# Reordering masks, row sums and transposes in the attention part of a fused attention and expert kernel

## The chip, the cores and the metric

The kernel runs on one core of a Trainium2 chip. The metric is the device time of one execution in microseconds (us), less is better. Within one group of times executions repeat within about 0.4%, but the kernel before has two groups that lie 1.3 us apart, and this matters below. Three chips took part in the experiments, and one of them is slower in the part of the kernel that the change does not touch; kernels are therefore compared with runs of the kernel before on the same chip, or by stretches of the trace that the slow part does not reach. On that chip some executions were in a slower state (over 1.5% above the fastest of the same kernel): 5 of 27 of the kernel before, 1 of 14 of its repeat, and 2 of 6 of the new loop with the old start. Ratios use fast runs alone.

## The reference, cut to what matters

The reference is attention with a local window of 96 keys and 8 global keys, over 4 batches of 8 heads, followed by an assignment of tokens to 8 experts and their two matmuls.

```python
def _attn_ref(q, k, v, n_global, n_local):          # q, k, v: 4 x 8 x 768 x 64
    scores = scale * np.matmul(q, k.transpose(0, 1, 3, 2))
    ...                                             # bias: slope of the head times distance
    scores = np.where(keep, scores, -1000000000.0)
    a = np.exp(scores - np.max(scores, axis=-1, keepdims=True))
    a = a / (np.sum(a, axis=-1, keepdims=True) + 1e-09)
    return np.matmul(a, v)

def _moe_ref(x, w_gate, w1, w2):                    # x: 3072 tokens x 512
    logits = x @ w_gate                             # each token goes to one expert, by logit,
    ...                                             # and each expert takes at most 384
    h = np.maximum(x[mask] @ w1[e], 0.0)
    out[mask] = h @ w2[e]
```

## The kernel before

The eight half-batches of four heads are called u = 0 to 7. One period of the main loop handles one u, that is two head pairs n = 2u and 2u+1. The keys of a half-batch fall into three groups g = 0, 1, 2. TensorE computes the scores of a group, ScalarE applies the exponential, VectorE (DVE) multiplies by a mask of bias and window, TensorE then forms the product with the values and the row sums. In these traces an engine takes its instructions in the order of the program text, even where it has to wait (VectorE stands 8.8 us at masks in the four steady periods, as the prediction shows), so the text is the schedule.

```python
def blocks(key, src, g):                            # key or query transpose, 0.97 us on DVE
    t = tring[len(tTs) % 4]
    nc.vector.transpose(out=t, in_=src[:, :, 32 * g : 32 * g + 32])

def kA_out(u, g, i0=0, last=True):                  # key copies, one large, two small
    small_copy = nc.gpsimd.tensor_copy if u < 3 else nc.scalar.copy
    nc.scalar.copy(out=kA[:, i0:i1, 8:128]..., in_=...)
    small_copy(out=kA[:, :, 0:8], in_=...)          # if i0 == 0
    small_copy(out=kA[:, i1, 8 : 8 + LASTK]..., in_=...)   # if last

def qT_out(u, g, c0=0, c1=32, dve=False):           # query copy, ScalarE or DVE
    copy = nc.vector.tensor_copy if dve else nc.scalar.copy
    ...
def build_W(h):                                     # mask weights of one head
    nc.scalar.activation(Wm[:, h, :], Dm, AF.Exp, scale=-slopes[h])

def expo(u, g, ps):                                 # exponential, one for each of two head pairs
    nc.scalar.activation(P[:, :, 0 : GW[g]], ps[w_][:, :, 0 : GW[g]], AF.Exp, scale=0.125)

def mask(n, g):                                     # DVE: P = P * Wm
    ...
def attend(n, g):                                   # TensorE: po += P, v ; av(n) does all three groups
    ...
def sums_out(n, pr):                                # DVE: LT = transpose of the row sums,
    nc.vector.transpose(out=LT2..., in_=pr...)      #      ri = 1/LT, Gb = product,
    ...                                             #      and after every fourth pair a reduce to logits
# one period of the loop, before (u = 2 .. 6, abridged)
ps = scores(u, 0); expo(u, 0, ps)
tok / tok_out of pair A-1                           # token transposes (TensorE), scaling (DVE)
kT(u + 1, 0); kT(u + 1, 1)
mask(2 * u, 0); mask(2 * u + 1, 0)                  # masks of the group just exponentiated
av(A); oT_out(A, 0); oT_out(A, 1)
pr = sums(A); kA_out x 2; qT(u + 1, 0); qT_out(u + 1, 0); sums_out(A, pr)
ps = scores(u, 1); expo(u, 1, ps)
qT(u + 1, 1); qT_out(u + 1, 1)
mask(2 * u, 1); mask(2 * u + 1, 1)
tok / tok_out of pair A
av(Bp); oT_out(Bp, 0); oT_out(Bp, 1)
ps = scores(u, 2); expo(u, 2, ps)
mask(2 * u, 2)
pr = sums(Bp); sums_out(Bp, pr)
mask(2 * u + 1, 2)
four pieces of deferred constants                   # some on GpSimd, some on DVE
```

The first two half-batches (the start) and the last one (u = 7, with the early token ids for one expert mixed in) are written out separately.

The softmax here doesn't subtract the row's maximum and nothing guards it: scores larger than these inputs give would overflow.

## Time and profile before

| | before |
|---|---|
| time, three runs | 258.96, 259.26, 260.93 us |
| the execution that was profiled | 260.64 us (span 258.8) |
| attention, first scores to first routing transpose (px) | 9.2 to 141.97 us |
| px to the end | 116.8 us |

The page lists the share of each engine and, in its part 4, the chain of work that ended last.

```profile
PE 239.3 (92%) x2931; PEld 178.4 (69%) x2943; DVE 166.0 (64%) x347; ACT 142.9 (55%) x233; POOL 92.4 (36%) x158
...
PE 35%; DVE 30%; ACT 11%; issue 9%; DMA 8%; POOL 4%; POOLq 0%; DVEq 0%; ACTq 0%
```

TensorE (PE) looks nearly full by its busy share, but 30% of the chain that sets the end runs through DVE, which is busy for 64% only. So DVE has idle time and is on the chain all the same: its order may hold others up. The waits that the prediction lists say where.

One more line matters for what follows. It is the busy time in a stretch of the trace of before (stretch, its length, then busy time and count of PE, PEld, DVE, ACT, POOL, then the granted TensorE clock, the DMA share and GB/s).

```profile
9.00:13.00 4.00, 3.80 (x47) 3.81 (x51) 3.22 (x6) 2.53 (x4) 0.95 (x4) 0.57 1.17 272
```

The clock of TensorE was 0.57 on average just as the first scores ran. ScalarE (fourth of the counts) was busy for 2.53 of 4 us there, because it had to wait for those scores.

### The profile page before, as it was taken

How to read it: one execution, taken by the hardware profiler on the slowest of the kernel's cores; microseconds unless marked ns; L12 is line 12 of the kernel's file. 1: busy time of each engine (PE TensorE's matmuls, PEld its weight loads, DVE VectorE, ACT ScalarE, POOL GpSimd, SP SyncE). 2: the span in 40 equal slices, each digit the busy share in tenths (PEclk: the TensorE clock that was granted, in tenths of full speed). 3: DMA queues.
4: the chain of work that ended last, by engine and by line, in shares of the span. 5: the costliest groups of instructions: out<-in, count | busy, mean ns of one | idle time of the engine just before them, and what ended most of it. 6: DMA issues, size and time to landing. Idle time of an engine off the chain costs nothing.

```text
span 258.8 us, 7066 instructions
## 1 busy us (share of the span) xinstructions
PE 239.3 (92%) x2931; PEld 178.4 (69%) x2943; DVE 166.0 (64%) x347; ACT 142.9 (55%) x233; POOL 92.4 (36%) x158
## 2 busy tenths in 40 slices
PE   8699998998999989998999999998999999999960
PEld 3577876887888868886788877765677775555520
DVE  3896999799896998969794787773232323223120
ACT  4699957869688697793332523323444442341600
POOL 6210400030180494006008401127884766732240
PEclk9799999999999999999999999999999999999997
DMA  7997396929969599976999999942599999992221
GB/s 263 332 285 118 122 252 169 270 30 262 234 175 274 116 251 231 169 186 91 203 212 212 149 186 212 242 126 88 97 221 252 260 252 260 235 262 98 81 84 47
DMA packets 52566, 49.24 MB, mean 190 GB/s; under 512 B 29744, under 2 KB 44080, under 8 KB 52528
## 3 DMA queue, kind: packets, MB, share of 16 engines
q0 software_dynamic: 15680, 26.22, 49.6%
q1 hardware_dynamic: 36848, 22.50, 33.6%
q8 instruction: 25, 0.41, 0.7%
q14 instruction: 13, 0.11, 0.1%
HBM read 56.05 MB, written 9.44 MB: 253 GB/s over the span
## 4 chain that ended last, share of the span: by engine, by line
PE 35%; DVE 30%; ACT 11%; issue 9%; DMA 8%; POOL 4%; POOLq 0%; DVEq 0%; ACTq 0%
DVE P L426 8%; DVE RT L332 8%; PE ph L1407 7%; PE po L1416 5%; PE ps L393 5%; DMA out_dram<-ot,idi 4%; ACT P L411 4%; ACT qT L358 4%; POOL out_dram L967 4%; PE poE L1010 3%; PE po L446 3%; DMA RT<-x_tok,idiE 2%; DVE x L532 2%; DVE LT L494 2%; PE phE L994 2%
## 5 line engine op out<-in xcount | busy, mean ns | idle before, releaser
L393 PE MATMUL ps<-qT,kA 32*128 32x215 f32 (+2 forms) x864 | 47.6, 342 | 2.4 <-ACT qT L358 2.1
L411 ACT ACTIVATE P<-ps 128x860 f32<-128x860 f32 (+1 forms) x46 | 39.1, 890 | 16.6 <-PE ps L393 15.7
L1410 ACT ACTIVATE hT<-ph 128x256 bf16<-128x256 f32 (+1 forms) x64 | 27.1, 423 | 38.3 <-PE ph L1407 36.3
L393 PEld LDWEIGHTS ps<-qT,kA 32*128 32x128 f32 x864 | 39.6, 189 | 9.3 <-issue 7.0
L446 PE MATMUL po<-P,v 128*64 128x215 f32 (+6 forms) x576 | 41.3, 293 | 0.3 <-DVE P L426 0.3
L446 PEld LDWEIGHTS po<-P,v 128*64 128x64 f32 x576 | 34.0, 136 | 8.3 <-issue 3.6
L426 DVE TENSOR_TENSOR P<-P,Wm 128x860 f32<-128x860 f32 (+1 forms) x32 | 32.9, 1045 | 8.0 <-ACT P L411 5.9
L332 DVE STREAM_TRANSPOSE RT<-RT 128x768 f32<-128x768 f32 x28 | 26.0, 957 | 3.5 <-DMA RT<-in_k_dram 3.4
L1423 DVE COPY ot<-po 128x512 f32<-128x512 f32 x18 | 12.4, 691 | 23.9 <-PE po L1416 23.1
L967 POOL DMA_INDIRECT out_dram<-ot,idi x19 | 18.7, 982 | 23.5 <-DVE ot L1423 18.2
L343 ACT COPY kA<-RT 128x720 f32<-128x720 f32 (+2 forms) x18 | 24.1, 1350 | 2.2 <-DVE RT L332 2.1
L1416 PEld LDWEIGHTS <-hT 128*128 128x128 bf16 x152 | 14.4, 98 | 15.5
L451 ACT COPY oT<-po 128x384 f32<-128x384 f32 x32 | 14.6, 483 | 16.2 <-PE po L446 16.2
L1407 PE MATMUL ph<-xT,w 128*128 128x384 bf16 (+1 forms) x160 | 23.4, 305 | 0.0
L1388 DVE COPY xT<-pxe 128x512 bf16<-128x512 bf16 x17 | 6.6, 420 | 26.0 <-PE pxe L1387 25.6
L476 PE MATMUL pr<-P,onesx 128*32 128x192 f32 (+11 forms) x384 | 22.6, 349 | 0.7 <-DVE x L532 0.7
L1416 PE MATMUL po<-w,hT 128*128 128x512 bf16 x99 | 22.8, 379 | 0.2
L959 POOL DMA_INDIRECT xe<-x_tok,idi x19 | 18.4, 967 | 9.8 <-issue 4.0
L1407 PEld LDWEIGHTS <-w 128*128 128x128 bf16 x160 | 15.7, 98 | 7.7
L476 PEld LDWEIGHTS pr<-P,onesx 128*32 128x32 f32 x384 | 18.4, 108 | 2.5 <-DVE x L532 0.8
L419 DVE TENSOR_TENSOR P<-P,Wm 128x860 f32<-128x860 f32 x16 | 16.4, 1055 | 4.0 <-ACT P L411 4.0
L524 PE MATMUL pk<-ident,oT 128*128 128x128 f32 x96 | 15.6, 285 | 3.2 <-DVE LT L494 3.2
(249 smaller groups left out, 339.5 us busy)
## 6 DMA issues: line engine op xcount, KB each, us to landing
w<-in_moe_w_dram POOLq DMA_DIRECT2D x10, 1024.0 KB, 10.6
v<-in_v_dram SPq DMA_DIRECT2D x32, 180.0 KB, 3.4
RT<-in_k_dram SPq DMA_DIRECT2D x7, 768.0 KB, 4.6
RT<-in_q_dram SPq DMA_DIRECT2D x7, 768.0 KB, 8.5
w_early<-in_moe_w_dram POOLq DMA_DIRECT2D x8, 512.0 KB, 7.2
x_tok<-x SPq DMA_DIRECT2D x32, 96.0 KB, 3.2
RT<-in_moe_w_dram POOLq DMA_DIRECT2D x2, 1024.0 KB, 16.1
w_early<-in_k_dram SPq DMA_DIRECT2D x1, 768.0 KB
```

Source lines behind the costliest of these rows:

```text
L332: nc.vector.transpose(out=t, in_=src[:, :, 32 * g : 32 * g + 32])
L343: nc.scalar.copy(out=kA[:, i0:i1, 8:128].rearrange("p i (c j) -> p i c j", j=NJ), in_=t[:, i0 * NC5 : i1 * NC5, :].rearrange("p (i c) j -> ...
L393: nc.tensor.matmul(heads[a][:, o : o + w], lhsT=kA[r, gd, i, :], rhs=qTt[r, gd, KT * i : KT * i + w], start=(gd == 0), stop=(gd == 1), ski ...
L411: nc.scalar.activation(P[:, :, 0 : GW[g]], ps[w_][:, :, 0 : GW[g]], AF.Exp, scale=0.125)
L426: tt(out=P[:, :, 0 : GW[g]], in0=P[:, :, 0 : GW[g]], in1=Wm[:, h0 : h0 + 2, lo : lo + GW[g]], op=ALU.mult)
L446: nc.tensor.matmul(po[n][bk][64 * t : 64 * t + 64, a - QB * bk : z - QB * bk], lhsT=v7[:, t, i, :], rhs=P[:, t, o + a - q0 : o + z - q0], ...
L476: nc.tensor.matmul(o_, lhsT=l_, rhs=r_, start=first[gq], stop=True, skip_group_check=True)
L959: ins = nc.gpsimd.indirect_dma_start(out=xe, out_offset=None, in_=x_tok[:, :], in_offset=bass.IndirectOffsetOnAxis(ap=idi[:, s : s + 1], a ...
L967: s = nc.gpsimd.indirect_dma_start(out=out[:, :], out_offset=bass.IndirectOffsetOnAxis(ap=ids, axis=0), in_=ot, in_offset=None)
L1407: nc.tensor.matmul(ph[:, 0 : 128 * ns], lhsT=w1_of(e)[:, kc, 128 * fc : 128 * fc + 128], rhs=xT_e[:, kc, 0:ns, :].rearrange("p t n -> p (t ...
L1410: nc.scalar.activation(hT[:, fc, 0 : 128 * ns], ph[:, 0 : 128 * ns], AF.Relu)
L1416: nc.tensor.matmul(po, lhsT=hT[:, fc, 128 * j : 128 * j + 128], rhs=w2_of(e)[:, fc, :], start=(fc == 0), stop=(fc == NFC - 1))
```

## The change

The intent is to run each mask when its exponential has long ended instead of right behind it, so that DVE never stands still in front of a mask while transposes and row-sum work queue up behind. The masks of a group move up to one period later (the table SLOT says which run where), the row-sum chain follows the sums directly, and the DVE constants leave the loop but for u = 4. The start is reordered likewise: weight builds move, four filler matmuls go, key copies come in halves. The masks (12,2) and (13,2), a mask being written as (pair, group), move from u = 6 into the last period, where the mask (14,0), the scores of group 1 and the row-sum chain of pair 12 move too.

```diff
-            small_copy = nc.gpsimd.tensor_copy if u < 3 else nc.scalar.copy
+            small_copy = nc.gpsimd.tensor_copy if u < 4 else nc.scalar.copy
 ...  the start, u = 0 and 1 (cut)
+            build_W(3)
+            kT(1, 0)
+            kA_out(1, 0, last=False)
+            kT(1, 1)
             expo(0, 0, ps)
-            kT(1, 0)
-            kT(1, 1)
+            qT(1, 0)
             mask(0, 0)
-            nc.vector.tensor_copy(out=ident_bf, in_=ident)
 ...
-            warm(4)
 ...  the loop
+            SLOT = {u: ([(2 * u - 2, 1), (2 * u - 2, 2)], [], [], [(2 * u - 1, 1), (2 * u - 1, 2)], [(2 * u, 0), (2 * u + 1, 0)])
+                    for u in range(3, NU - 1)}
+            SLOT[2] = ([(2, 1)], [], [(3, 0)], [(3, 1), (3, 2)], [(4, 0)])
+            SLOT[3] = ([(4, 1), (4, 2)], [], [(5, 0)], [(5, 1), (5, 2)], [(6, 0), (7, 0)])
+            SLOT[6] = ([(10, 1), (10, 2)], [(11, 1)], [], [(11, 2), (12, 0)], [(13, 0), (12, 1), (13, 1)])
             for u in range(2, NU - 1):
                 ps = scores(u, 0)
                 expo(u, 0, ps)
+                if u == 2:
+                    build_W(6)
+                    build_W(7)
+                masks(u, 0)
                 ...  tok, kT
-                    mask(2 * u, 0)
-                    mask(2 * u + 1, 0)
                 av(A)
                 ...  oT_out
+                for g in range(2):
+                    kA_out(u + 1, g)
                 pr = sums(A)
                 sums_out(A, pr)
+                masks(u, 2)
                 ps = scores(u, 1)
                 expo(u, 1, ps)
+                qT(u + 1, 0)
+                qT_out(u + 1, 0)
+                masks(u, 3)
+                qT(u + 1, 1)
                 ...  tok, tok_out, av(Bp), oT_out
+                if u > 2:
+                    qT_out(u + 1, 1)
                 ps = scores(u, 2)
                 expo(u, 2, ps)
-                    mask(2 * u, 2)
+                masks(u, 4)
                 pr = sums(Bp)
                 sums_out(Bp, pr)
-                mask(2 * u + 1, 2)
 ...  the last period, u = 7
             e1_pe()
+            mask(12, 2)
             e2_cut()
-            mask(14, 0)
+            ps = scores(u, 1)
             attend(12, 2)
             ...
+            mask(13, 2)
             pr = sums(12)
-            sums_out(12, pr)
-            ps = scores(u, 1)
             expo(u, 1, ps)
             e5_pe()
             e6_count()
+            sums_out(12, pr)
 ...
+            mask(14, 0)
             mask(14, 1)
```

## The prediction

> **What bounds the kernel now.** I read the page's forty slices first. The last 117 us (routing and experts, from about 142 us) are not touched, and the waits of PE there add up to about 1 us. The attention stretch, 9 to 142 us, is what the change rewrites. I cut it at the first scores matmul of each head group u (each "period" handles two head pairs), and asked for busy times by stretch. Columns: stretch, length, busy time of PE, PEld, DVE, ACT, POOL, granted clock, DMA share, GB/s.
>
> ```profile
> 33.23:50.36 17.13, 15.76 (x260) 12.96 (x261) 15.67 (x24) 13.05 (x20) 0.00 (x0) 1.00 0.91 233
> 50.36:67.11 16.75, 15.91 (x261) 13.11 (x261) 15.04 (x24) 13.58 (x19) 2.22 (x8) 1.00 0.74 163
> 67.11:83.17 16.06, 16.06 (x261) 13.42 (x260) 13.78 (x24) 13.04 (x19) 6.56 (x13) 1.00 0.92 217
> 83.17:99.96 16.79, 15.70 (x262) 13.14 (x261) 15.12 (x27) 13.36 (x19) 10.55 (x21) 1.00 0.90 223
> 99.96:116.04 16.08, 16.08 (x262) 13.41 (x261) 13.27 (x21) 13.07 (x19) 1.74 (x3) 1.00 0.92 172
> ```
>
> Periods u=2 to 6 alternate between 16.1 and 16.8 us, the first takes 17.1. PE seems full, but it is not: from the timeline of u=4, scores for groups 0, 1, 2 take 1.67, 1.67, 1.88 us unblocked, the two attention products 2.45 each, the two row-sum sets 1.67 each, the four token transposes 1.6 together: 15.06 us. Each period loses 1.0 to 2.1 us. Where, the waits of u=3 to 6 tell (waiter <- releaser: us, times, longest):
>
> ```profile
> DVE P L426 <- ACT P L411: 4.8, 5, 1.3
> DVE P L419 <- ACT P L411: 4.0, 4, 1.6
> PE pk L524 <- DVE LT L494: 1.8, 2, 1.1
> PEld ps L393 <- ACT P L411: 1.3, 4, 0.4
> ```
>
> DVE stands 8.8 us in four periods at a mask whose exponential is not ready; the work behind that mask comes late, and PE's second token transpose waits 1.1 us for DVE's LT transpose, which must free a PSUM buffer. This is seen in the odd periods only (DVE has a reduce of 0.85 us there and in u=5 five small constant instructions). The even periods are set by something else, ScalarE, as its timeline of u=4 shows: from the end of the first attention product (72.43) no gap until the last exponential ends at 83.5, which is what the scores of the next period wait for.
>
> ```profile
> 72.56 0.48 ACT L451 COPY oT<-po 128x384 f32<-128x384 f32 x1 [0.66 <-PE po L446]
> 72.94 1.54 ACT L343 COPY kA<-RT 128x720 f32<-128x720 f32 x1
> ...
> 76.47 1.55 ACT L358 COPY qT<-RT 128x768 f32<-128x768 f32 x1
> 77.93 1.65 ACT L411 ACTIVATE P<-ps 128x860 f32<-128x860 f32 x2
> 79.47 1.56 ACT L358 COPY qT<-RT 128x768 f32<-128x768 f32 x1
> 80.92 0.87 ACT L451 COPY oT<-po 128x384 f32<-128x384 f32 x2
> 81.66 1.87 ACT L411 ACTIVATE P<-ps 128x862 f32<-128x862 f32 x2
> ```
>
> So there are two bounds: the ScalarE chain (every period) and DVE's order (odd periods, u=2 and the start).
>
> **What the Trainium skill says.** "PSUM — Partial Sum Buffer", Engine vs sequencer instructions: ScalarE and VectorE queues are strict FIFO. The trace agrees: 8.8 us of DVE idle stands before masks while later work was ready. "Perfetto Trace Analysis", Identifying the Most-Contended Engine: matmul busy time is not a measure of headroom. It agrees: u=4 shows PE 16.06 of 16.06 us busy with 15.06 of work. "TensorE: Matmul & The Clock Gate", What's actually happening: the array's clock is throttled after idleness. The trace has 0.50 from 10 to 12 us; the change drops the four filler matmuls at 16.0 us (1.04 us), after which real work follows.
>
> **The change part by part.** PE's order in u=2 to 6 is unchanged, and no large instruction is added or removed. All times below are hand-scheduled from durations in the trace: mask 0.97, key/query transpose 0.88, token scaling 0.47, sums chain on DVE 1.0 (1.94 with the reduce), key copy 1.77 (1.42 without the two small ones), query copy 1.46 on ACT and 0.8 on DVE.
>
> *Steady periods.* Masks move up to one period later: those of groups 1 and 2 run when their exponential has long ended. DVE then never waits for ScalarE, and its sums chain starts when PE's row sums end. With the scores of a period effectively starting at 0: sums(A) ends 6.6, LT is done at 7.3, PE's second token transpose is due at 8.7: that wait (1.1) is gone. What remains is ScalarE: scores, token transposes and first product 4.96 (83.53 to 88.49 in the trace), 0.13 to the copy, then the same copies and exponentials, 72.56 to 81.66 = 9.10, and the last exponential 1.67 (it lasted 1.87 as its second half waited for a P buffer): 15.86. One query copy moves behind the middle exponential, which frees the scores of group 2 earlier, but the last exponential still comes after the same ScalarE work. So even periods gain only 16.06 - 15.86 = 0.2. In odd periods the reduce delays the first key transpose to 5.7 to 5.8, 0.3 to 0.45 late for ScalarE; in u=3 the masks of the second head also end 0.75 us too late for PE. That makes 16.4 (u=3) and 16.3 (u=5). I measure periods at the end of the last exponential: before 16.47, 16.06, 16.77, 16.1; after 16.4, 15.86, 16.3, 15.86. Sum **-1.0**.
>
> *Start (u=0, 1).* The mask of group 2 moves from 17.92 to 17.0 (one transpose is taken out ahead of it, the bf16 identity copy of 0.23 leaves): the first product ends at 18.95, not 20.0. A mask (head pair 2, group 1) and three weight builds (0.7 each: one into a gap of ScalarE at 10.96, two into u=2) leave u=1. LT is ready when the token transposes want it (wait of 0.65 us gone), and the second product ends at 27.6 instead of 29.4. The ScalarE work (key copies, two weight builds) then holds the exponential of u=1, group 2 until 31.25, so that u=2 starts effectively at 31.3; before it was 33.67 (33.84 minus the little that had run). **-2.35**.
>
> *u=2.* Small key copies go to GpSimd (0.35 us per half off ScalarE) and one query copy to DVE. I get 16.2, PE waiting 0.75 for a mask; before 51.1 - 33.67 = 17.4. **-1.2**.
>
> *u=7.* Masks (12,0),(12,1),(13,0),(13,1) are done in u=6, which ends no later for it; but (12,2), (13,2), (14,0) lie on the chain to the early token ids. Before, ids came 18.6 us after the period's start; I sum 18.8 after it, then the same 6.9 us of id-gather DMA. **+0.2**.
>
> Sum: -1.0 - 2.35 - 1.2 + 0.2 = -4.35 us, all on the path (each moves the start of the next period; the part after 142 us shifts as a whole). 259.26 - 4.35 = 254.9; I say 255.0.
>
> **The rivals.** (a) *PE becomes the bound:* if ScalarE can absorb its chain (its busy sum is 13.0 of 16.1), periods fall to 15.1 to 15.4 and the time to about 251. For it: PE's unblocked sum. Against it: the idle ScalarE time, 3 us per period, lies before the first product ends, and nothing in the change moves ScalarE work there. (b) *New waits eat it:* masks now come just before the product that uses them; by my schedule they are only 0.0 to 0.2 us early in even periods, so small delays fall on PE; each period might lose 0.3 to 0.5 again, giving 257. (c) *Loads:* the last query transpose moves 1.5 us later, so its buffer's next load is issued later; 8.5 us to landing (median) against about 12 until it is needed, so it should stay hidden; at the start DMA is saturated until 22 us (share 1.0 and more), and keys of u=2 are wanted 7 us earlier. If they are late, the start's gain of 2.35 shrinks to about 1, giving 256.5. (d) *Key copies on GpSimd suffer from DVE:* "SBUF — State Buffer", Who interferes with whom, calls the shared port pair an exclusive lock; a 1-column GpSimd copy here took 0.19 us at 56.05 and 2.36 at 72.43, overlapping DVE work. They have 10 us, so nothing.
>
> **Range and chances.** 255.0 is the sum; 252.7 takes half of (a), 257.3 is (b) or (c). 2% faster means below 254.1, only 0.9 us under my figure, and a hand schedule is good to 1 us or 2. Faster by over 2%: 0.34; within: 0.65; slower: 0.01.
>
> **What would show it.** Right: DVE no longer waits for ACT at the masks (8.8 us before, below 1 after); the PE wait for LT gone; periods 3 to 6 between 15.8 and 16.4 with scores of u+1 still waiting for the last exponential (wait of the first scores 0.8 us and more); u=2 starting near 31.3, u=7 near 112; the id gather 18.8 us later. Wrong: even periods below 15.5 (ScalarE was not the bound), PE waits for masks in every period, or DVE waits for key loads at 20 us.

## The result, and the profile after

The changed kernel took 256.11 us (median of four runs, 255.99 to 256.53), against 259.86 us (258.96 to 260.93, four runs) for the kernel before. The ratio is 0.9857, with a 95% interval of 0.9811 to 0.9902: about 1.4% faster, within 2%. A ratio here and below is the mean time of one kernel's fast runs over that of the other's fast runs of the same rounds, so it is not quite the ratio of the medians quoted. The profiled span fell from 258.8 to 254.2 us.

The same two parts of the page, for the changed kernel:

```profile
PE 236.9 (93%) x2939; PEld 175.1 (69%) x2939; DVE 166.8 (66%) x348; ACT 140.6 (55%) x230; POOL 96.0 (38%) x162
...
PE 46%; DVE 15%; DMA 13%; issue 9%; ACT 8%; POOL 4%; SPq 1%; POOLq 0%; DVEq 0%; ACTq 0%
```

Busy times hardly moved, as they should when only the order changes. What moved is the chain: DVE's part of it fell from 30% to 15%, and TensorE's rose from 35% to 46%.

The stretches from one first scores matmul to the next, of u = 2 and u = 6, in the columns described above:

```profile
30.57:47.51 16.94, 16.12 (x262) 12.82 (x260) 14.51 (x22) 12.34 (x16) 6.24 (x14) 1.00 0.71 179
...
95.77:111.69 15.92, 15.77 (x261) 13.13 (x261) 14.89 (x22) 12.97 (x19) 1.68 (x3) 1.00 0.98 205
```

Period u = 2 now begins 2.66 us earlier (30.57 for 33.23), and u = 7 begins 4.35 us earlier (111.69 for 116.04). Now the waits between 50 and 116 us, the steady periods, as in the prediction (waiter <- releaser: us in total, times, longest):

```profile
ACT P L416 <- PE ps L398: 7.8, 5, 1.6
...
DVE LT L499 <- PE pr L486: 3.8, 5, 0.9
PEld ps L398 <- ACT P L416: 2.7, 6, 0.6
...
PEld po L451 <- DVE P L424: 1.1, 1, 1.1
```

The two rows of DVE waiting at a mask for ScalarE, 8.8 us before, are gone, and so is TensorE's wait of 1.8 us for LT. DVE now waits for TensorE's row sums, which is the right way round. The scores still wait for the last exponential (2.7 us on the weight-load queue, 1.3 before), so ScalarE is still a bound. Its timeline of u = 4, from the end of the first product on:

```profile
69.49 0.48 ACT L456 COPY oT<-po 128x384 f32<-128x384 f32 x1 [0.66 <-PE po L451]
69.87 1.50 ACT L348 COPY kA<-RT 128x720 f32<-128x720 f32 x1
...
73.36 1.66 ACT L416 ACTIVATE P<-ps 128x860 f32<-128x860 f32 x2
74.91 1.56 ACT L363 COPY qT<-RT 128x768 f32<-128x768 f32 x1
76.36 0.88 ACT L456 COPY oT<-po 128x384 f32<-128x384 f32 x2
77.10 1.58 ACT L363 COPY qT<-RT 128x768 f32<-128x768 f32 x1
78.56 1.69 ACT L416 ACTIVATE P<-ps 128x862 f32<-128x862 f32 x2
```

No instruction after the first shows a wait: the chain is gapless from 69.49 to 80.25 us, as it was before the change.

To see where the time went, I cut each trace at the end of the last exponential of a period. The first column is the end of that of u = 1 (the start); then come the lengths of periods 2 to 6, and then the time from there to px, the first routing transpose. From px to the end takes 116.8 us in both kernels (258.8 - 141.97 and 254.2 - 137.44). "Clock" is the granted clock between 9 and 13 us. The last two rows are second profiles of the same two kernels, which I come to below.

| trace | clock | u=1 ends | u=2 | u=3 | u=4 | u=5 | u=6 | to px | px |
|---|---|---|---|---|---|---|---|---|---|
| before | 0.57 | 33.33 | 17.70 | 16.44 | 16.06 | 16.78 | 16.08 | 25.58 | 141.97 |
| after | 1.00 | 30.92 | 16.95 | 16.53 | 15.85 | 16.24 | 15.92 | 25.03 | 137.44 |
| before, again (slower chip) | 1.00 | 32.06 | 17.71 | 16.45 | 16.09 | 16.78 | 16.06 | 26.42 | 141.57 |
| after, again | 0.57 | 31.09 | 16.94 | 16.52 | 15.87 | 16.26 | 15.91 | 25.26 | 137.85 |

### The profile page after: what moved, and what is told of

It is laid out like the page before. It is cut to its first block, busy times and chain, and to the rows that moved or that the text cites. A ratio compares the mean times of both kernels' runs of the same rounds, so it can differ in the third digit from the quotient of the medians.

```text
span 254.2 us, 7081 instructions
## 1 busy us (share of the span) xinstructions
PE 236.9 (93%) x2939; PEld 175.1 (69%) x2939; DVE 166.8 (66%) x348; ACT 140.6 (55%) x230; POOL 96.0 (38%) x162
## 4 chain that ended last, share of the span: by engine, by line
PE 46%; DVE 15%; DMA 13%; issue 9%; ACT 8%; POOL 4%; SPq 1%; POOLq 0%; DVEq 0%; ACTq 0%
PE ps L398 7%; PE ph L1419 7%; PE po L451 7%; PE po L1428 5%; DMA x_tok<-x 4%; DMA out_dram<-ot,idi 4%; PE pr L481 4%; POOL out_dram L979 4%; DVE P L431 3%; PE poE L1022 3%; DVE RT L337 3%; PE pk L529 3%; ACT qT L363 3%; ACT P L416 3%; DMA RT<-in_q_dram 2%
## 5 line engine op out<-in xcount | busy, mean ns | idle before, releaser
L398 PE MATMUL ps<-qT,kA 32*128 32x215 f32 (+2 forms) x864 | 45.7, 334 | 4.0 <-ACT qT L363 2.8
L398 PEld LDWEIGHTS ps<-qT,kA 32*128 32x128 f32 x864 | 37.9, 185 | 11.0 <-issue 6.2
L451 PE MATMUL po<-P,v 128*64 128x215 f32 (+6 forms) x576 | 42.5, 294 | 1.8 <-DVE P L424 1.4
L451 PEld LDWEIGHTS po<-P,v 128*64 128x64 f32 x576 | 33.1, 136 | 10.9 <-DVE P L431 2.4
L979 POOL DMA_INDIRECT out_dram<-ot,idi x19 | 18.6, 981 | 23.2 <-DVE ot L1435 16.1
L1428 PE MATMUL po<-w,hT 128*128 128x512 bf16 x104 | 23.8, 379 | 0.0
L537 DVE TENSOR_TENSOR x<-pk,ri 128x384 bf16<-128x384 f32 x32 | 16.5, 546 | 0.6 <-PE pk L529 0.4
L424 DVE TENSOR_TENSOR P<-P,Wm 128x860 f32<-128x860 f32 x16 | 16.4, 1036 | 0.0
```

Of the source, the lines that this page charges most:

```text
L398: nc.tensor.matmul(heads[a][:, o : o + w], lhsT=kA[r, gd, i, :], rhs=qTt[r, gd, KT * i : KT * i + w], start=(gd == 0), stop=(gd == 1), ski ...
L451: nc.tensor.matmul(po[n][bk][64 * t : 64 * t + 64, a - QB * bk : z - QB * bk], lhsT=v7[:, t, i, :], rhs=P[:, t, o + a - q0 : o + z - q0], ...
L979: s = nc.gpsimd.indirect_dma_start(out=out[:, :], out_offset=bass.IndirectOffsetOnAxis(ap=ids, axis=0), in_=ot, in_offset=None)
L1428: nc.tensor.matmul(po, lhsT=hT[:, fc, 128 * j : 128 * j + 128], rhs=w2_of(e)[:, fc, :], start=(fc == 0), stop=(fc == NFC - 1))
```

## The experiments

Twelve runs were made, in three groups of four, each group on one chip; two of them repeat the two kernels unchanged. All gave correct results. The medians of the kernel before in the three groups were 266.16 us (first four labels below; 266.03 us of its fast runs), 260.18 us (next four) and 260.33 us (last four). The first chip's routing and expert part took 122 to 124.5 us instead of 116.8; its attention periods agree with the other chips to 0.03 us.

### The start without the new loop

The new start (u = 0, 1) stands in front of the old loop. Three masks of pair 3, two of pair 2 and two weight builds, which the new start has left out, must come somewhere, so they run at the head of u = 2.

```diff
 ...  new start, then the old loop with
+                if u == 2:
+                    build_W(6); build_W(7)
+                    for n, g in ((2, 1), (2, 2), (3, 0), (3, 1), (3, 2)):
+                        mask(n, g)
```

> The new order of the first two periods, then the old loop (the masks of head pairs 2 and 3 that the new start leaves over are run at the head of u=2). Theory (the start gains by itself, because the scores of u=1 and the second product wait less): the scores of u=2 start near 30.6 us as in the changed kernel, u=2 then takes about 1 us longer than before (one more mask and two weight builds in it), u=3 to 6 last 16.4, 16.1, 16.8, 16.1 us as before; in all 1.5 to 2.3 us faster than before. Rival (the start only moves work into u=2, nothing is gained): u=3 starts at 50.4 us as before, 0 to 0.5 us faster.

Measured: 266.05 us, ratio 1.0013 [0.9994, 1.0032], so no gain at all. The last exponential of u = 1 ended at 30.81 us, as in the changed kernel, but u = 2 then took 20.21 us instead of 17.7. The timeline of u = 2 in this kernel shows why.

```profile
35.39 1.06 DVE L426 TENSOR_TENSOR P<-P,Wm 128x860 f32<-128x860 f32 x1 [1.60 <-ACT Wm L399]
...
38.29 1.01 DVE L532 TENSOR_TENSOR x<-pk,ri 128x384 bf16<-128x384 f32 x2
...
38.90 1.64 PE L476 MATMUL pr<-P,onesx 128*32 128x384 f32 x18 [3.05 <-DVE x L532]
```

DVE runs two masks, waits 1.60 us for a weight build of ScalarE, and runs three more. The token scaling comes after them at 38.29 us, and TensorE stands 3.05 us because its row sums need the buffer that the scaling frees. In this execution the stall has a second cost: the granted clock then falls to 0.50 from 40 to 43 us, and the first 18 row-sum matmuls take 1.64 us where the same work takes 1.25 us in the changed kernel. (It was the slowest of the 15 executions, 269.11 us, mostly for a longer part behind px; whether the others had the low clock in u = 2 is not shown.) The theory that the start is worth some 2 us by itself is refuted in this form: the new start pushes work into u = 2, and only a loop that spreads it gets the gain. This is the strict order of a queue that the prediction cited, now on the losing side.

### The loop without the new start

```diff
 ...  old start, new loop and last period with
-            SLOT[2] = ([(2, 1)], [], [(3, 0)], [(3, 1), (3, 2)], [(4, 0)])
+            SLOT[2] = ([], [], [], [], [(4, 0)])        # the old start has done these masks
-                if u == 2: build_W(6); build_W(7); ... mask(2, 2)
```

> The old start, the new loop order from u=2. Theory: u=2 to 6 last about 16.1, 16.5, 15.9, 16.2, 15.9 us from end of the last exponential to the next, against 17.4, 16.4, 16.1, 16.8, 16.1 before; with the last period in all 1.9 to 2.5 us faster than before. Rival (PE is freed in the loop and the steady periods carry most of the gain): over 3 us faster.

Measured: 263.77 us (263.42 us of its four fast runs), ratio 0.9899 [0.9847, 0.9951], about as expected. In the trace u = 1 ends at 33.20 us (with a cold clock), u = 2 takes 16.43 (16.1 was expected), and u = 3 to 6 take 16.52, 15.88, 16.21 and 15.91 us, the same as in the changed kernel within 0.03 us. The loop's gain stands without the new start. It also says what the start is worth on top of the new loop: u = 2 ends at 49.63 us here and at 48.03 us in the changed kernel, both with a cold clock, so 1.60 us.

### Constants back in the loop

```diff
     def later_dve(f):
-        late_dve.append(f)
+        late.append(f)
 ...
-                if u == 4:
-                    late_dve.pop(0)()               # and the same for the rest, after expo(u, 2)
```

> The changed kernel, but the small constant instructions of VectorE (0.5, 0.7 and 0.95 us) back at the ends of u=2, 3 and 4 instead of inside u=4. Theory (in odd periods DVE's order sets the first key copy; in u=4 it has 0.9 us to spare twice): u=3 and u=4 0.1 to 0.5 us longer, u=5 within 0.2 of the changed kernel because u=4 then ends with DVE free earlier; 0.3 to 0.8 us slower than the changed kernel. Rival (moving the constants is what shortens the odd periods): 1.5 to 2 us slower than the changed kernel, u=5 at 16.8 or more.

Measured: 261.89 us, ratio 0.9861 [0.9826, 0.9896]. Against the changed kernel the periods changed by -0.16 (u=2), +0.21, +0.80, -0.34, 0.0: +0.5 us in all. The sum is as expected, its distribution is not: u = 4 pays and u = 5 gets some of it back. (The total cannot show 0.5 us: the interval contains the changed kernel's ratio.) The timelines of DVE show that this run did not put the constants back where they had been. In the kernel before, five of them stand behind the reduce at the head of u = 5 and hold DVE for 0.93 us (86.47 to 87.40):

```profile
84.75 0.85 DVE L517 TENSOR_REDUCE Lb<-Gb 128x48 f32<-128x384 f32 x1
...
86.47 0.15 DVE L214 TENSOR_SCALAR rowe<-rowe 90x1 f32<-90x1 f32 x1
...
87.22 0.26 DVE L220 TENSOR_SCALAR TriE<-res_e,rowe 90x90 bf16<-90x90 f32 x1
```

In this run they stand, with others, at the head of u = 4, and hold it for 1.54 us (65.69 to 67.23), while u = 5 has none:

```profile
65.69 0.25 DVE L191 TENSOR_SCALAR res_i<-res_i 128x192 int32<-128x192 int32 x1
...
67.05 0.27 DVE L219 TENSOR_SCALAR TriE<-res_e,rowe 90x90 bf16<-90x90 f32 x1
```

So the rival, that these few DVE instructions made most of u = 5's excess, is not refuted: at the head of u = 4 this run's constants cost 0.80 us, and u = 5 without any takes 15.90. With them back, u = 3 to 6 together take 65.21 us, against 65.36 before and 64.54 after; how the gain divides between masks and constants stays open.

### The kernel before, unchanged

> The kernel before, unchanged, for a second profile and as a measure of noise. In its first profile the granted clock was 0.50 from 10 to 12 us and the first scores took 3.2 us; in the profile of the changed kernel 1.00 and 1.9 us. If that is chance and not the change, this run may show a clock of 1.00 there and a span about 0.5 to 1.3 us shorter than 258.8, u=2 starting near 32.5 to 33.2 us; if it comes with the kernel, 0.50 again. Ratio 1.00 within 0.4%.

Measured: 265.56 us, ratio 0.9996 [0.9972, 1.0019] to the kernel before on the same chip. All its periods repeat within 0.03 us. But u = 1 ended at 32.06 us instead of 33.33, and the busy time of the same stretch shows a different clock:

```profile
9.00:13.00 4.00, 3.76 (x72) 3.31 (x72) 3.96 (x7) 3.83 (x6) 1.10 (x3) 1.00 1.12 272
```

With a clock of 1.00 instead of 0.57, ScalarE is busy for 3.83 of the 4 us and not for 2.53. Two further traces whose start is the old one agree: 33.20 us with a clock of 0.57 (the new loop with the old start), and 32.04 us with 1.00, on one of the faster chips (the kernel before with GpSimd copies, below). So a cold clock at the start costs the kernel before about 1.2 us (1.14 to 1.29), whatever the chip. I return to this after the other runs.

### The small key copies on GpSimd, in the changed kernel

```diff
-            small_copy = nc.gpsimd.tensor_copy if u < 4 else nc.scalar.copy
+            small_copy = nc.gpsimd.tensor_copy
```

> The changed kernel with the small key copies (0.19 + 0.18 us per half on ScalarE, 0.74 us per period) on GpSimd in all periods. Theory (after the change ScalarE's chain from the end of the first product to the last exponential sets u=3 to 6): these periods become 0.5 to 0.74 us shorter each, 15.2 to 15.9 us, in all 2.0 to 2.8 us faster than the changed kernel, and the first scores of a period no longer take 2.1 to 2.5 us but below 2.0. Rival (PE's own 15.1 us plus small waits for masks is the bound): below 0.5 us. Rival (DVE's order): below 0.5 us, with PE waiting for masks.

Measured: 255.73 us, ratio 0.9828 [0.9795, 0.9861]. The periods u = 3 to 6 were 16.52, 15.56, 15.84 and 15.47: shorter by 0.0, 0.29, 0.40 and 0.45 us than in the changed kernel. The two key copies of a period, with their small ones, had lasted 3.49 us together and now take 2.88, so 0.6 us left ScalarE. About half to three quarters of it reached the periods u = 4 to 6, less than expected: in u = 4 the last exponential took 1.92 us for 1.69, probably because its second half waited for a buffer that the row sums read. In all 1.14 us against the 2.0 to 2.8 expected. That ScalarE sets u = 4 and 6 is confirmed, and so is that it does not set u = 3.

### The same edit in the kernel before

```diff
-            small_copy = nc.gpsimd.tensor_copy if u < 3 else nc.scalar.copy
+            small_copy = nc.gpsimd.tensor_copy
```

> The kernel before with the same small key copies on GpSimd. Theory (before, ScalarE set the even periods and DVE's order the odd ones): u=4 and 6 0.4 to 0.7 us shorter (15.4 to 15.7), u=3 and 5 hardly (0 to 0.2); in all 0.9 to 1.7 us faster than before, less than what the same edit gives after the change. Rival (ScalarE set all periods before): 0.7 us in each of five periods, 3 us and more.

Measured: 258.66 us, ratio 0.9953 [0.9936, 0.9971]. Periods u = 2 to 6: -0.23, +0.17, -0.53, -0.08, -0.61 us. Freeing ScalarE helps the even periods and leaves u = 3 and 5: for the kernel before it is shown that ScalarE sets u = 4 and 6 and does not set u = 3 and 5. That DVE's order sets these two is not shown by this run; it rests on the waits.

### More work for DVE, and more for ScalarE

Two kernels add work of no use to the changed kernel, in u = 3 to 6: two memsets on DVE before each row-sum chain, or two copies on ScalarE behind the key copies.

```diff
+                if u > 2:                            # the DVE kernel, in two places of the loop
+                    for _ in range(2):
+                        nc.vector.memset(spacer, 0.0)
```

> The changed kernel with about 0.5 us of VectorE fill ahead of each of the two sums chains in u=3 to 6 (4 us of DVE work in all). Theory (DVE has 0.8 to 0.9 us to spare before each sums chain): nothing in even periods, 0 to 0.5 us in u=3 and 5 where the reduce and the constants use it up: 0 to 1.0 us slower. Rival (DVE is still the bound): 3 to 4 us slower.

```diff
+                if u > 2:                            # the ScalarE kernel, after kA_out
+                    for _ in range(2):
+                        nc.scalar.copy(out=spacer, in_=Dm[:, 0:184])
```

> The changed kernel with two small ScalarE copies (about 0.5 us together; their length is read from the trace) after the key copies in u=3 to 6. Theory (ScalarE's chain is the bound there): every one of the four periods longer by the whole length, about 2 us slower in all. Rivals (PE or DVE): 0 to 0.5 us slower.

The groups of instructions give the size of the added work in each kernel (busy us, mean ns of one, then idle time before them). The DVE kernel:

```profile
L818 DVE MEMSET spacer<- 128x184 f32 x8 | 1.7, 212 | 0.4
L850 DVE MEMSET spacer<- 128x184 f32 x8 | 1.7, 212 | 0.4
```

The ScalarE kernel:

```profile
L817 ACT COPY spacer<-Dm 128x184 f32<-128x184 f32 x8 | 2.8, 346 | 0.1
```

So each period got 0.85 us of DVE work (four times 0.212), or 0.69 us of ScalarE work (twice 0.346).

| added to | u=3 | u=4 | u=5 | u=6 | time | ratio |
|---|---|---|---|---|---|---|
| DVE, 0.85 us a period | +0.02 | +0.01 | +0.47 | +0.01 | 256.81 | 0.9876 [0.9848, 0.9904] |
| ScalarE, 0.69 us a period | +0.11 | +0.70 | +0.32 | +0.65 | 257.44 | 0.9897 [0.9869, 0.9924] |

This is the clearest evidence of the study. In u = 4 and 6 the ScalarE work comes through in full and the DVE work not at all: ScalarE is the bound there, and DVE has 0.85 us to spare. In u = 5 each costs about half, so both are near the bound. In u = 3 neither of the added loads matters much, although the period is the longest of the four; for ScalarE this misses the expectation, which was the whole length in every period.

### A better order for u = 2, 3 and 5

In u = 2 the masks (3,1) and (3,2) move ahead of the middle scores, and the reduce of batches 0 and 1 moves from the head of u = 3 and 5 (in the row-sum chain) behind the last masks of the period.

```diff
-            SLOT[2] = ([(2, 1)], [], [(3, 0)], [(3, 1), (3, 2)], [(4, 0)])
+            SLOT[2] = ([(2, 1)], [], [(3, 0), (3, 1), (3, 2)], [], [(4, 0)])
 ...
-            elif j == NPAIR - 1:                     # in sums_out
-                ... reduce of the batch ...
+            elif j == NPAIR - 1 and b == 2:
+                logits(b)
 ...
                 masks(u, 4)
+                if u in (3, 5):
+                    logits((u - 3) // 2)
```

> The changed kernel with two moves on VectorE and no work added: in u=2 masks (3,1) and (3,2) go ahead of the query transpose (PE waited 0.69 us for (3,1) there); the logit reduce of 0.85 us of batches 0 and 1 goes from the head of u=3 and u=5 to the end of these periods, where DVE was seen idle for 0.92 us. Theory (DVE's order is what makes u=2, 3 and 5 longer than 15.9): u=2 15.8 to 16.4 instead of 16.95, u=3 15.9 to 16.2 instead of 16.53, u=5 15.85 to 15.95 instead of 16.24, u=4 and 6 unchanged; 1.1 to 2.1 us faster than the changed kernel. Rival (these periods are long for another reason, such as PE's clock or loads): below 0.4 us.

Measured: 255.11 us, ratio 0.9816 [0.9784, 0.9848]. u = 2 fell from 16.95 to 16.47 us and u = 5 from 16.24 to 15.89; u = 3 stayed at 16.53 (15.9 to 16.2 was expected). The reduce of 0.85 us therefore helped to set u = 5 but not u = 3. What sets u = 3 stands in the two timelines. First the changed kernel:

```profile
54.63 0.58 DVE L499 STREAM_TRANSPOSE LT<-pr 128x384 f32<-128x384 f32 x1 [0.36 <-PE pr L486]
...
55.68 1.05 DVE L431 TENSOR_TENSOR P<-P,Wm 128x860 f32<-128x860 f32 x1
56.65 0.97 DVE L337 STREAM_TRANSPOSE RT<-RT 128x768 f32<-128x768 f32 x1
57.54 1.02 DVE L424 TENSOR_TENSOR P<-P,Wm 128x860 f32<-128x860 f32 x1
...
58.61 1.94 PE L451 MATMUL po<-P,v 128*64 128x144 f32 x28 [0.69 <-DVE P L424]
```

And the kernel of this experiment, half a microsecond earlier:

```profile
54.09 0.58 DVE L508 STREAM_TRANSPOSE LT<-pr 128x384 f32<-128x384 f32 x1 [1.24 <-PE pr L486]
...
58.08 1.94 PE L451 MATMUL po<-P,v 128*64 128x144 f32 x28 [0.69 <-DVE P L424]
```

Without the reduce DVE merely waits longer for the row sums: 1.24 us for 0.36, a difference of 0.88, which is the reduce. From the row sums on, the LT chain, the mask (5,0), a query transpose and the mask (5,1) follow without a gap, and TensorE waits 0.69 us for (5,1) as before. In u = 4 to 6 the mask of the second pair's group 0 has run in the period before; only SLOT[2] and SLOT[3] have it in their third place, and only u = 2 and u = 3 have this wait of 0.69 us. That this placement costs u = 3 its 0.69 us is what the timelines say; a kernel with (5,0) moved was not run.

### That order and the GpSimd copies together

```diff
 ...  the two edits above: small_copy = nc.gpsimd.tensor_copy, and the order of u = 2, 3 and 5
```

> The same and the small key copies on GpSimd in all periods. Theory (both bounds are relieved together, so that the second no longer hides the first's gain): u=3 to 6 at 15.4 to 15.6 us each; 2.5 to 3.5 us faster than the changed kernel, 252.5 to 253.6 us where that takes 256.1. Rival (the gains overlap, no more than the better of the two): 1.1 to 2 us faster.

Measured: 254.94 us, ratio 0.9802 [0.9771, 0.9833], the best of all. The changed kernel took 256.26 us on the same chip. The profiled span was 252.4 us, 2.2 us below the changed kernel's 254.6 on this chip (which had the cold clock), and the medians differ by 1.3 us. That is less than expected and lies in the rival's range, but not for the rival's reason. The periods u = 2 to 6 are 16.47, 16.67, 15.56, 15.56 and 15.46 us, 1.77 us less in all than in the changed kernel; alone the order gave 0.83 and the copies 1.14, so the gains nearly add up. What is missing is u = 3, expected at 15.4 to 15.6, which neither edit shortens. Whether it beats the kernel before by over 2% is not settled, since the interval includes 0.98.

### The mask (12,2) ahead of the token scaling, in the last period

```diff
             attend(12, 1)
+            mask(12, 2)                              # ahead of the token scaling of pair 11
 ...
-            mask(12, 2)
             e2_cut()
```

> The changed kernel, but in the last period mask (12,2) again ahead of the token scaling, as before the change. Theory (the last period became shorter because the token scaling no longer stands behind a mask, so that PE gets to its last row sums earlier; the ids come no earlier): ids within 0.15 us of the changed kernel's 18.85 after the last exponential of u=6, PE's start of the last row sums 0.3 to 0.7 us later (4.7 us after the ids in the changed kernel, 5.4 before), the end 0 to 0.6 us later. Rival (ScalarE or the id gather alone set it): PE's last row sums no later, end within 0.1 us.

The edit restores the order of the mask and the token scaling of pair 11, not the old place of the mask: before the change it ran in u = 6. Measured: 256.23 us, ratio 0.9858 [0.9827, 0.9888], the same as the changed kernel on this chip. The period u = 7 grew by 0.24 us and the ids came 0.24 us later (within 0.15 was expected), but the last row sums came 4.41 us after the first gather was issued, exactly as in the changed kernel (before: 4.94). This order does not explain what u = 7 gained.

### The changed kernel, again

> The changed kernel again, for a second profile and a ratio on the same chip as the others. Ratio 0.984 to 0.989; u=2 to 6 as in its first profile within 0.1 us (16.95, 16.53, 15.85, 16.24, 15.92); last exponential of u=1 at 30.9 us if the clock is 1.00 from 10 to 12 us, at 31.3 if it is 0.50.

Measured: 256.26 us, ratio 0.9853 [0.9822, 0.9884]. Its periods are in the table above and repeat within 0.03 us. Its stretch from 9 to 13 us:

```profile
9.00:13.00 4.00, 3.91 (x48) 3.86 (x52) 3.97 (x6) 3.75 (x5) 0.99 (x4) 0.57 1.16 271
```

This execution had the cold clock, and yet u = 1 ended at 31.09 us, only 0.17 us later than in the first profile. Two of its variants, the constants back in the loop and the small copies on GpSimd, had a low clock that lasted longer (0.83 and 0.50 still between 13 and 14 us, where this one has 1.00) and ended u = 1 at 31.33 and 31.31 us, 0.4 us later. ScalarE is busy for 3.75 of the 4 us: the new start gives it a weight build and a key copy while the cold scores run, and before it had nothing there.

### The two groups of times

The clock also sorts the times. The runs of the kernel before list their mean granted clock. On the chip of the last group, the four runs with 0.987 or more took 259.01 to 259.33 us, and the five with 0.986 or less took 260.33 to 260.74. Divided in the same way, the second group's chip has 11 runs with a median of 259.35 and 16 with one of 260.68 (one of the 16, 259.66 us at 0.986, has a time of the other kind). So the groups lie about 1.3 us apart, which is what the traces give for the cold start (1.14 to 1.29). For the changed kernel the first result had two runs at 0.992 (255.99 and 256.01) and two at about 0.98 (256.20 and 256.53): 0.4 us apart. The link between clock at the start and group is shown in the profiled runs; for the others it is an inference from the mean clock.

## Why the prediction was right or wrong

The time (256.1 for 255.0) lies in the range and in the class that was called likeliest. The steps, compared where both traces had the cold clock (before, and the changed kernel again):

| step | predicted | cold against cold |
|---|---|---|
| start | -2.35 | 31.09 - 33.33 = -2.24 |
| u = 2 | -1.2 | 16.94 - 17.70 = -0.76 |
| u = 3 to 6 | -1.0 | 64.56 - 65.36 = -0.80 |
| u = 7 to px | +0.2 | 25.26 - 25.58 = -0.32 |
| sum | -4.35 | -4.12 |

**The subtraction at the end** is the step that explains the miss of 1.1 us. "259.26 - 4.35" took a sum worked out on the profiled execution from a median of other executions. The profiled one took 260.64 us and had the cold clock at its start; two of the three runs behind 259.26 belong to the faster group. Taken from its own execution, the same sum gives 260.64 - 4.35 = 256.3, against 256.1 measured. The start's -2.35 is right for a cold start only. Between two warm executions it is 30.92 - 32.06 = -1.14 (32.04 on a faster chip), because half of what the new order gains there is that it hides the cold clock. The prediction had seen the 0.50 on the page and did not ask whether every execution has it.

The table counts between ends of exponentials. The prediction let u = 2 of the kernel before begin at 33.67, 0.34 us after that end; counted from 33.33 its first two figures are -2.0 (31.3 - 33.33) and -1.5 (16.2 - 17.70). So the start gained 0.2 us more than predicted, and u = 2 about 0.7 us less.

**The steady periods** went as worked out: 16.53, 15.85, 16.24 and 15.92 us for the predicted 16.4, 15.86, 16.3 and 15.86. The gain is mostly that of u = 5 (16.78 to 16.24); u = 3 gained nothing (16.44 to 16.53), where 0.07 was predicted. The bounds hold too: the loads of 0.69 and 0.85 us show ScalarE as the bound of the even periods, and the PE wait of 0.69 us in u = 3 is the "0.75 us too late" of the prediction. DVE's 8.8 us of waits at masks are gone, and the four periods together are 0.80 us shorter: most of that idle time held nobody up. Part of the 0.80 us may come from the DVE constants that left the heads of the periods, which the prediction did not count; no run separates the two. Rival (a), TensorE as the bound, is refuted for the even periods by the same load. Rival (b), new waits in every period, did not come: only u = 2 and u = 3 have one of 0.69 us.

**u = 2** was over-estimated: 16.95 for 16.2. The prediction counted one wait of 0.75 us for a mask, and the trace has it:

```profile
40.87 1.01 DVE L424 TENSOR_TENSOR P<-P,Wm 128x860 f32<-128x860 f32 x1
41.80 1.20 DVE L431 TENSOR_TENSOR P<-P,Wm 128x862 f32<-128x862 f32 x1
41.94 2.09 PE L451 MATMUL po<-P,v 128*64 128x144 f32 x28 [0.69 <-DVE P L424]
42.17 1.22 POOL L200 TENSOR_SCALAR eofs_l<-eofs_bf 1x120 bf16<-1x120 bf16 x1
```

The sum of the rest came 0.7 us short. With both masks ahead of the middle scores u = 2 still took 16.47, so 0.48 of it belongs to the order of the masks. Another part is GpSimd work beside the second mask, which lasted 1.20 us. In the run with the constants back in the loop DVE and ScalarE have the same instructions in u = 2, but GpSimd has nothing to do there after 38.62 us, and the same mask is shorter:

```profile
42.21 1.05 DVE L431 TENSOR_TENSOR P<-P,Wm 128x862 f32<-128x862 f32 x1
```

That period took 0.16 us less (16.79). It happens once more in u = 3 of the order and the copies together: the mask in this place took 1.20 us beside GpSimd work for 1.05 in the changed kernel, and the period 16.67 for 16.53. In u = 2 the two parts were not removed together, and about 0.1 us stays open. Rival (d), key copies that suffer on GpSimd, did not come: in u = 2 the small copies took 0.27 to 0.28 us each and the last ended at 37.57 us, ten before the next scores, and moving more of them to GpSimd shortened the periods. What the prediction did not have is the reverse, a mask that suffers.

**u = 7** had the wrong sign. The token ids came 18.85 us after the last exponential of u = 6, against 18.69 before, so the part about the masks (+0.2) was right. The failing term is "the same 6.9 us of id-gather DMA". From the ids to px it took 6.89 us before and 6.18 after. The timelines of TensorE and GpSimd at the end of attention show two things that px waits for. The kernel before:

```profile
135.50 1.49 POOL L664 DMA_INDIRECT RT<-x_tok,idiE  x1 [13.81 <-DVE idiE L659]
...
140.44 1.41 PE L476 MATMUL pr<-P,onesx 128*32 128x384 f32 x24
...
141.97 0.59 PEld L902 LDWEIGHTS <-RT 128*128 128x128 bf16 x8 [0.33 <-DMA RT<-x_tok,idiE]
```

The changed kernel:

```profile
131.55 1.63 POOL L669 DMA_INDIRECT RT<-x_tok,idiE  x1 [14.46 <-DVE idiE L664]
...
135.96 1.41 PE L481 MATMUL pr<-P,onesx 128*32 128x384 f32 x24
...
137.43 0.58 PEld L914 LDWEIGHTS <-RT 128*128 128x128 bf16 x8 [0.28 <-DMA RT<-x_tok,idiE]
```

px needs the gathered rows and also TensorE, which is busy with the last row sums. These end 6.35 us after the gather's issue before (141.85 - 135.50) and 5.82 us after the change (137.37 - 131.55). The gather itself varies: px followed its issue by 6.47 us before, and by 5.75 to 6.59 us in the changed kernel and its variants, in some with no wait for the DMA left. So the 6.9 us were not a DMA time but the later of two things, and the change brought one of them 0.5 us forward. Which of the moves in the last period did this is open; it was not the order of the mask (12,2) and the token scaling. Nor is the size of the gain settled: on the two faster chips the time to px is 25.58 and 25.53 us in two traces with the old last period, and 24.89 to 25.59 us in eight with the new one. Rival (c), late loads at the start, did not come either: u = 1 ended at 30.92 and 31.09 us in the two profiles of the changed kernel, and the prediction had 31.25.

**The start and the loop are not additive parts.** The prediction gave the start -2.35 as a part of its own, with the work that it leaves to u = 2 counted there. In front of the old loop it gained nothing; in front of the new one, 1.60 us by the end of u = 2 with a cold clock.

**Small slips.** The durations that the prediction lists are distances from one start to the next: it has 0.97 for a mask, and the traces list about 1.05 as the time of one. Half of (a) from 255.0 is 253.0, not 252.7.

## What to carry to other kernels

When an engine with time to spare is on the critical chain, look for the instruction at the head of its queue that waits, and move it to where its input is long ready; then add a known load to one engine at a time, because a period that grows by exactly that load has its bound there and one that does not grow has it elsewhere. Take a predicted saving from the time of the execution that was profiled, not from a median of others, and check first whether a clock or a state at the start differs between them. A time "from ids to the next matmul" was here the later of two arrivals, so it did not carry over as a constant: ask what else the matmul needs.

## What the Trainium skill lacked or had wrong

- "TensorE: Matmul & The Clock Gate", What's actually happening, states that the window is free-running and that the number of cold matmuls varies from run to run. This case agrees in so far as the same kernel had a clock of 0.57 or of 1.00 between 9 and 13 us; whether the window is free-running no run here shows. The page puts the price at under 1% of a typical span, which agrees as well (about 1.2 of 258.8 us, 0.5%). What it lacks is that the price depends on the other engines: 1.14 to 1.29 us of the kernel before, 0.2 to 0.4 us of the changed one, in which ScalarE had other work ready.
- "Perfetto Trace Analysis", Identifying the Most-Contended Engine, says to optimise the engine of the highest occupancy first (TensorE is to be judged otherwise). In u = 6 of the changed kernel DVE is busy for 14.89 of 15.92 us and ScalarE for 12.97, and yet 0.85 us of added DVE work changed nothing there and 0.69 us of ScalarE work lengthened it by 0.65 us. Occupancy did not name the bound of this periodic chain; no page gives the added load as a test.
- No page has a figure for how far such a mask slows beside GpSimd work; it would belong to "SBUF — State Buffer", Who interferes with whom. Here the same mask of u = 2 took 1.20 us beside a GpSimd instruction and 1.05 us in the run that had none there.
